# Twelve matmuls on a zero tile, placed in TensorE's waits between the attention steps of the first block

## The chip, the cores and the metric

The kernel runs on one core of one Trainium2 chip. The traces show five engines of it, which run side by side (busy for 95, 41, 38 and 22% of the first span below, the fifth only issues) and wait for each other: TensorE (PE: matmuls, and PEld: its weight loads), VectorE (DVE), ScalarE (ACT), GpSimd (POOL) and SyncE (SP, which issues the transfers). The metric is the device time of one launch in microseconds (us), and lower is better. "Span" is the length of one profiled execution from its first to its last instruction; in the pairs below it is about 1.8 us shorter than the time.

## The reference

The input is q, k, v of 8 batches, 8 heads, 576 positions, 64 columns. Attention is done in chunks of 64 positions, and its result goes through a bilinear feed-forward layer:

```python
scores = scale * np.matmul(q_c, k_c.transpose(0, 1, 2, 4, 3))   # chunks of 64
attn = softmax(scores)
x = np.matmul(attn, v_c)          # as 4608 tokens x 512
out = ((x @ w_a) * (x @ w_b)) @ w_out      # w_a, w_b: 512 x 1536, w_out: 1536 x 512
```

## The kernel before

Tokens are handled in 9 blocks of 512, each of two units of 256. A unit of attention is a chain of steps: transposes of q and k, `scores`, exp on ScalarE, `sums` (a matmul by ones), ln and exp(-x) on ScalarE (the reciprocal of the sum), `values`, and a multiply on VectorE that writes the tile xT. The projections of a block (`ab_step`) read xT. In the steady state attention of a later unit is woven between the projections of an earlier block. For block 0 there is nothing to weave it into: both of its units must be done first, and each step waits for another engine.

```python
def ab_step(K, ft, c0=0, c1=BLK):
    ...
    for n in ("wb", "wa"):
        ps[n] = bank()[:, :c1 - c0]
        for kt in range(NKT):                       # 4 matmuls, 128x512 for a whole block
            nc.tensor.matmul(ps[n], w_ab[n, i][:, kt, o:o + 128], xT[:, kt, c0:c1],
                             start=(kt == 0), stop=(kt == NKT - 1))
    ...
# the start of the program, in the order in which each engine runs it
for i in range(NWP - 1):
    cast_ab(i)                 # POOL casts a pair of weight tiles
    if i < 2:
        load_ab(i + 3)
scores(0)
transpose_pe(1)
sums(0)
scores(1)
values(0)
sums(1)
values(1)
load(2, "qk")
load_ab(5)
...
cast(2, "qk")                  # POOL; unit 2's transposes need it
cast_ab(5)
...
for ft in range(NFT):          # block 0, 12 steps of 8 matmuls
    ab_step(0, ft)
    if ft == 7:
        transpose_pe(2)
    if ft == 8:
        slot(2)                # scores of unit 2
    if ft == 10:
        slot(None, 2)          # sums and values of unit 2
```

The softmax here doesn't subtract the row's maximum and nothing guards it: scores larger than these inputs give would overflow.

## Time and profile before

| | before |
|---|---|
| time, median of the first 3 runs | 330.01 us (329.94 to 330.35) |
| span of the profiled execution | 329.1 us |
| TensorE busy | 311.4 us, 95% |
| block 0's first projection matmul starts | 19.65 us |
| from there to the recorded rise of the clock, at 24.19 us | 4.54 us |

The first two lines are from part 1 and part 4 of the profile's page (busy time of each engine; the chain of work that ended last, by engine). The third is the page's row of granted TensorE clock over 40 slices of the span.

```profile
PE 311.4 (95%) x2712; PEld 157.4 (48%) x2712; DVE 133.9 (41%) x209; ACT 126.7 (38%) x224; POOL 73.7 (22%) x76
...
PE 93%; ACT 3%; DMA 1%; DVE 1%; issue 0%; SPq 0%
...
PEclk9999999999999999999999999999999999999999
```

TensorE is the engine to look at, and it is nearly always busy. So one looks at when it waits, and at how fast it goes. Below, the waits of TensorE: who ended the wait, the total in us, how often, the longest.

```profile
PE ps L156 <- DVE q_raw L144: 5.4, 1, 5.4
PE ps L278 <- DVE xT L239: 3.8, 2, 2.7
PE ps L186 <- ACT qkt L164: 1.6, 2, 1.4
```

The longest xT wait, 2.7 us, is the one just before block 0. The timeline of TensorE shows it in place. The columns are start, duration from the first start to the last end, line, output and inputs, shapes, number of instructions, and in brackets the idle time before and what ended it.

```profile
11.72 0.64 PE L201 MATMUL ps<-E,ones 64*64 64x512 bf16 x4
13.59 0.64 PE L186 MATMUL ps<-qkt 64*64 64x64 bf16 x32 [1.23 <-DVE qkt L164]
...
15.36 1.12 PE L201 MATMUL ps<-E,ones 64*64 64x512 bf16 x4 [0.70 <-ACT E L194]
...
19.65 1.87 PE L278 MATMUL ps<-xT,wb_162 128*128 128x512 bf16 x4 [2.74 <-DVE xT L239]
21.31 1.91 PE L278 MATMUL ps<-xT,wa_164 128*128 128x512 bf16 x4
23.02 1.61 PE L278 MATMUL ps<-xT,wb_162 128*128 128x512 bf16 x4
24.47 1.03 PE L278 MATMUL ps<-xT,wa_164 128*128 128x512 bf16 x4
25.33 1.03 PE L278 MATMUL ps<-xT,wb_170 128*128 128x512 bf16 x4
...
35.69 0.61 PE L156 MATMUL ps<-identity,q_raw 128*128 128x128 bf16 x8
...
36.58 1.03 PE L278 MATMUL ps<-xT,wb_186 128*128 128x512 bf16 x4
...
45.99 0.60 PE L278 MATMUL ps<-xT,wb_162 128*128 128x256 bf16 x4 [1.11 <-DVE xT L239]
```

Read the starts, not the durations: the groups overlap (the one at 19.65 lasts 1.87 us, and the next starts 1.66 us after it). The groups of four at 19.65, 21.31 and 23.02 are 1.66 to 1.71 us apart, which is 0.42 to 0.43 us for each matmul. From 24.47 on the groups are 0.86 us apart, 0.216 us each. Same shape, same operands, half the rate. The clock row says 9 (that is 90% or more) throughout and does not show this. The trace also keeps a list of the changes of the granted clock. It begins here only at 24.19 us, with a rise to full speed, and the clock row counts what lies before the first entry as full: it gives 1.00 from 20.8 to 24.2 us, where the matmuls are 0.42 to 0.43 us apart. Times of a rise or fall of the clock below are entries of that list.

### The profile page before, as it was taken

The numbers are of one execution on the slowest core, as the hardware profiler recorded it, in microseconds if no ns is written. First come the engines' busy times: TensorE is split into PE (matmuls) and PEld (weight loads), VectorE is DVE, ScalarE is ACT, GpSimd is POOL, SyncE is SP. The second block draws the span as 40 slices with busy tenths as digits, with TensorE's granted clock in tenths as the row PEclk, the third lists the DMA queues.
The fourth block names the chain that finished last, engine by engine and source line by source line (L and its number), as shares of the span: only waits on it lengthen the run. The fifth ranks groups of instructions, "written<-read, shape, count | busy, mean of one in ns | idle before, by whom it ended". The sixth has DMA issues, their size and how long they took to land.

```text
span 329.1 us, 6671 instructions
## 1 busy us (share of the span) xinstructions
PE 311.4 (95%) x2712; PEld 157.4 (48%) x2712; DVE 133.9 (41%) x209; ACT 126.7 (38%) x224; POOL 73.7 (22%) x76
## 2 busy tenths in 40 slices
PE   2669989999999999999999999999999999999994
PEld 1424558776444444444444444444444444444441
DVE  3423454554443434343434343444344434433331
ACT  1633567257352525252525252525252524212200
POOL 1575556632222232132232211200000000000000
PEclk9999999999999999999999999999999999999999
DMA  8999899998979998999988918911120112012114
GB/s 241 320 383 293 225 371 257 276 214 197 173 198 248 228 224 192 225 210 253 203 207 211 231 34 147 241 31 34 42 54 3 34 34 64 1 32 63 35 32 96
DMA packets 139166, 53.91 MB, mean 164 GB/s; under 512 B 114560, under 2 KB 132992, under 8 KB 139136
## 3 DMA queue, kind: packets, MB, share of 16 engines
q1 hardware_dynamic: 139136, 53.49, 68.2%
q8 instruction: 21, 0.34, 0.4%
q14 instruction: 9, 0.07, 0.1%
HBM read 37.75 MB, written 9.44 MB: 143 GB/s over the span
## 4 chain that ended last, share of the span: by engine, by line
PE 93%; ACT 3%; DMA 1%; DVE 1%; issue 0%; SPq 0%
PE ps L278 57%; PE ps L294 28%; PE ps L201 2%; PE ps L156 2%; PE ps L186 2%; PE ps L230 1%; DMA k_in<-in_k_dram 1%; ACT rs L216 1%; ACT ln L212 1%; ACT qkt L164 1%; DVE xT L239 0%; DVE k_raw L144 0%; DVE o_sb L302 0%; ACT E L194 0%; SPq L129 0%
## 5 line engine op out<-in xcount | busy, mean ns | idle before, releaser
L286 ACT CAST b_sb<-ps 128x512 bf16<-128x512 f32 (+1 forms) x120 | 64.4, 546 | 142.6 <-PE ps L278 141.4
L287 DVE TENSOR_TENSOR ab_sb<-ps,b_sb 128x512 bf16<-128x512 f32 (+1 forms) x120 | 75.6, 637 | 94.1 <-PE ps L278 89.7
L294 PEld LDWEIGHTS <-ab_sb 128*128 128x128 bf16 x432 | 42.3, 98 | 50.1
L302 DVE COPY o_sb<-ps 128x512 f32<-128x512 f32 x36 | 24.9, 692 | 56.8 <-PE ps L294 56.8
L239 DVE TENSOR_TENSOR xT<-ps,rs 128x512 bf16<-128x512 f32 x36 | 23.4, 687 | 32.3 <-ACT rs L218 27.6
L144 POOL CAST q_raw<-q_in 128x1024 bf16<-128x1024 f32 x17 | 17.7, 1042 | 60.3 <-DMA q_in<-in_q_dram 52.0
L212 ACT ACTIVATE ln<-ps 128x512 f32<-128x512 f32 x36 | 19.9, 596 | 26.4 <-PE ps L201 26.4
L144 POOL CAST k_raw<-k_in 128x1024 bf16<-128x1024 f32 x17 | 17.7, 1042 | 47.9 <-DMA k_in<-in_k_dram 47.7
L278 PE MATMUL ps<-xT,wb_162 128*128 128x512 bf16 (+1 forms) x80 | 20.2, 378 | 3.8 <-DVE xT L239 3.8
L144 POOL CAST v_raw<-v_in 128x1024 bf16<-128x1024 f32 x18 | 18.8, 1042 | 17.7 <-DMA v_in<-in_v_dram 13.3
L294 PE MATMUL ps<-wo_437,ab_sb 128*128 128x512 bf16 x72 | 21.4, 379 | 0.0
L294 PE MATMUL ps<-wo_443,ab_sb 128*128 128x512 bf16 x72 | 21.4, 379 | 0.0
L294 PE MATMUL ps<-wo_433,ab_sb 128*128 128x512 bf16 x72 | 21.4, 379 | 0.0
L294 PE MATMUL ps<-wo_439,ab_sb 128*128 128x512 bf16 x72 | 21.4, 379 | 0.0
L294 PE MATMUL ps<-wo_441,ab_sb 128*128 128x512 bf16 x72 | 21.4, 379 | 0.0
L294 PE MATMUL ps<-wo_435,ab_sb 128*128 128x512 bf16 x72 | 21.4, 379 | 0.0
L194 ACT ACTIVATE E<-ps 128x512 bf16<-128x512 f32 x36 | 19.3, 587 | 1.8 <-PE ps L186 1.8
L278 PE MATMUL ps<-xT,wa_164 128*128 128x512 bf16 (+1 forms) x80 | 19.7, 370 | 0.0
L278 PE MATMUL ps<-xT,wb_186 128*128 128x512 bf16 (+1 forms) x80 | 18.9, 359 | 0.0
L278 PE MATMUL ps<-xT,wb_170 128*128 128x512 bf16 (+1 forms) x80 | 18.9, 359 | 0.0
L278 PE MATMUL ps<-xT,wb_182 128*128 128x512 bf16 (+1 forms) x80 | 18.8, 358 | 0.0
L278 PE MATMUL ps<-xT,wb_409 128*128 128x512 bf16 (+1 forms) x80 | 18.8, 358 | 0.0
(60 smaller groups left out, 324.5 us busy)
## 6 DMA issues: line engine op xcount, KB each, us to landing
out_dram<-o_sb SPq DMA_DIRECT2D x72, 128.0 KB, 2.4
v_in<-in_v_dram SPq DMA_DIRECT2D x32, 256.0 KB, 4.2
q_in<-in_q_dram SPq DMA_DIRECT2D x23, 256.0 KB, 3.9
k_in<-in_k_dram SPq DMA_DIRECT2D x23, 256.0 KB, 3.7
wst<-in_moe_w_b_dram SPq DMA_DIRECT2D x6, 512.0 KB, 7.3
wst<-in_moe_w_a_dram SPq DMA_DIRECT2D x6, 512.0 KB, 8.0
wst<-in_moe_w_out_dram SPq DMA_DIRECT2D x6, 512.0 KB, 7.2
q_in<-in_q_dram SPq DMA_DIRECT2D x4, 512.0 KB, 5.3
```

The source lines that it names most:

```text
L144: eng.tensor_copy(out=raw[n, U], in_=staged.pop((n, U)))
L156: nc.tensor.transpose(tp[:, i, m, :], src[:, i, 2 * m:2 * m + 2, :].rearrange("p j d -> p (j d)"), identity,)
L186: nc.tensor.matmul(sc[j][cl * 64:cl * 64 + 64, m, g, :], t[j * 64:j * 64 + 64, 1, g, m, cl * 64:cl * 64 + 64], t[j * 64:j * 64 + 64, 0, g, ...
L194: nc.scalar.activation(out=E_of[U][:, j], in_=sc[j], func=AF.Exp, scale=scale)
L201: nc.tensor.matmul(sm[cl][j * 64:j * 64 + 64, :], ones[cl * 64:cl * 64 + 64, :], E[cl * 64:cl * 64 + 64, j].rearrange("p m g s -> p (m g s)"),
L212: nc.scalar.activation(out=ln[:, cl].rearrange("p m n -> p (m n)"), in_=sm[cl], func=AF.Ln)
L239: nc.vector.tensor_tensor(out=x_tiles[K][:, :, c0:c0 + 128], in0=av[cl].rearrange("p m g s -> p m (g s)"), in1=rs[:, cl], op=MULT,)
L278: nc.tensor.matmul(ps[n], w_ab[n, i][:, kt, o:o + 128], xT[:, kt, c0:c1], start=(kt == 0), stop=(kt == NKT - 1),)
L286: nc.scalar.copy(out=b_sb[:, :c1 - c0], in_=ps["wb"])
L287: nc.vector.tensor_tensor(out=ab_tiles[K][:, ft, c0:c1], in0=ps["wa"], in1=b_sb[:, :c1 - c0], op=MULT)
L294: nc.tensor.matmul(o_ps, ab_tiles[K][:, ft, tg * 128:tg * 128 + 128], w_out[ft], start=(ft == 0), stop=(ft == NFT - 1),)
L302: nc.vector.tensor_copy(out=o_sb, in_=o_ps)
```

## The change

The intent is to keep TensorE's clock up through the waits of block 0's attention, so that block 0's projections begin at full speed. The result of the added matmuls is read by nobody. `bank()` takes one of the program's eight PSUM buffers, in which matmuls leave their results. In the prediction below, "cold" means at the slow rate and "warm" at the fast one.

```diff
+    warm_in = consts.tile([128, 512], BF16)
+    nc.gpsimd.memset(warm_in, 0.0)
+    warm_ps = []
+    def keep_warm(n):
+        if not warm_ps:
+            warm_ps.append(bank())
+        for _ in range(n):
+            nc.tensor.matmul(warm_ps[0], identity, warm_in, start=True, stop=True)
@@
         sums(0)
+        keep_warm(3)
         scores(1)
         values(0)
+        keep_warm(2)
         sums(1)
         values(1)
+        keep_warm(7)
         load(2, "qk")
```

## The prediction

> **What bounds the kernel.** TensorE: 311.4 of 329.1 us busy (page, part 1), 93% of the chain that ended last. Its waits (waits view, TensorE) sum to 13.1 us, all before 19.65 us but for 1.1 us at 45.99. So from block 0 on it is a TensorE stream; time is saved only by starting block 0 sooner or streaming it faster.
>
> **The slack aimed at.** Block 0's first matmuls (128x512) start 0.43 us apart (timeline: groups of four at 19.65, 21.31, 23.02). From 24.47 us the same instruction goes every 0.216 us. About eleven run at half speed, until about 24.2 us. Shapes and buffers are the same, so it is the array's clock, although the granted-clock row says 1.00 throughout. [...]TensorE idles 2.74 us before 19.65 (waiting for xT), then is slow for 4.6 us. Cost: (24.2-19.65)/2 = 2.3 us, all critical.
>
> **What the change adds.** Twelve 128x512 matmuls (0.43 us each cold, 0.216 warm), a PSUM bank held until block 0, a Pool memset in Pool's idle stretch (1.3-7.7 us). Against the old timeline:
> - Three after the sums of unit 0: 12.36 to 13.64, into a wait that ended at 13.59 (DVE copies). Delay at most 0.1 us.
> - Two after the values of unit 0: 14.7 to 15.55. The sums of unit 1 began at 15.36, but their second matmul needs the second exp, done at 15.80. No net delay.
> - Seven after the values of unit 1 (16.9): until 19.9 cold, 18.4 warm, into the wait until 19.65. The ScalarE chain (16.47 to 19.60) is untouched. Delay 0 to 0.25 us.
> - The held bank makes half of unit 0's values wait for a ScalarE ln ending about 14.16: about 0.1 us.
>
> With them TensorE is nearly continuously busy from 11.7 us[...]. Attention before it is bound by ScalarE and DVE and gains 0 to 0.2 us; block 0 starts at about 19.5 and streams at 0.216 us from its first matmul.
>
> **What is given back.** With block 0 about 2.2 us early, transposes of unit 2 (35.69 before) move to 33.5, while k_raw of unit 2 is cast until 34.12 (POOL timeline, DMA-fed): about 0.3 us stall. The last wa cast ends at 38.08 against a need at 39.2; v_raw of unit 2 at 39.89 against 40.4; w_out at 55.6 against 62. These hold, narrowly. Net gain about 2.0 us.
>
> **Prediction:** 328.0 us, 8 in 10 between 327.2 and 329.5. Faster by over 2%: 0.01; within 2%: 0.98; slower by over 2%: 0.01.
>
> **What would show it.** Right: block 0's first matmuls 0.216 us apart; busy time at the projection line about 2.3 us lower; block 0 begins at 19.4 to 19.8; a small new wait on k_raw at unit 2's transposes; everything after 46 us about 2 us earlier. Wrong: matmuls still 0.43 us apart after 19.65 (zeros or gaps don't count as activity; then 330.0 to 330.3); a slow stretch until about 21 (then 328.7); or the seven push block 0 past 19.9.
>
> **What could make it wrong.** [...]A new wait in block 0 for weights or loads could eat more than 0.3 us, since DMA is saturated until about 66 us.

"Before it" means before full speed. 2.3 us of slow matmuls, taken as about 2.2 us by which block 0 runs ahead, and less about 0.3 us of stall, came to about 2.0 us, from about 330.0 to 328.0 us. "Saturated" is the DMA share in the trace of the kernel before, as the windows view counts it: 1.11 from 9 to 27 us, 1.03 from there to 50 and 1.08 to 66, then 0.95 to 80.

## The result, and the profile after

| | before | after |
|---|---|---|
| time, median of 6 runs | 330.22 us (329.94 to 331.31) | 329.15 us (328.76 to 330.31) |
| ratio of fast runs | | 0.9965, 95% interval 0.9942 to 0.9987 |
| span of the profiled execution | 329.1 us | 327.5 us |
| block 0's first projection matmul starts | 19.65 us | 19.38 us |
| q transposes of unit 2 start | 35.69 us | 33.19 us |
| projections after those transposes start | 36.58 us | 35.02 us |
| block 1's first projection matmul starts | 45.99 us | 44.43 us |

All ratios here are the mean time of one kernel's fast runs over the mean time of the other's fast runs of the same rounds, so they are not quite the ratios of the medians. All timed runs quoted here count as fast, except one of **early_dma**, which is named there.

The lines that answer to those of before. First the page, then TensorE's waits, then its timeline (in the changed file the lines of the same code are numbered 12 higher; line 79 is the added matmul).

```profile
PE 311.8 (95%) x2724; PEld 157.2 (48%) x2724; DVE 133.9 (41%) x209; ACT 126.6 (39%) x224; POOL 74.0 (23%) x77
```

```profile
PE ps L290 <- DVE xT L251: 2.4, 2, 1.3
...
PE ps L168 <- POOL k_raw L156: 0.8, 1, 0.8
```

```profile
12.24 1.32 PE L79 MATMUL ps<-warm_in,identity 128*128 128x512 bf16 x3
13.56 0.45 PE L198 MATMUL ps<-qkt 64*64 64x64 bf16 x32
...
14.22 0.60 PE L79 MATMUL ps<-warm_in,identity 128*128 128x512 bf16 x2
...
16.38 1.69 PE L79 MATMUL ps<-warm_in,identity 128*128 128x512 bf16 x7
19.38 1.02 PE L290 MATMUL ps<-xT,wb_164 128*128 128x512 bf16 x4 [1.32 <-DVE xT L251]
20.24 1.03 PE L290 MATMUL ps<-xT,wa_166 128*128 128x512 bf16 x4
...
33.19 0.61 PE L168 MATMUL ps<-identity,q_raw 128*128 128x128 bf16 x8
34.56 0.62 PE L168 MATMUL ps<-identity,k_raw 128*128 128x128 bf16 x8 [0.76 <-POOL k_raw L156]
35.02 1.03 PE L290 MATMUL ps<-xT,wb_188 128*128 128x512 bf16 x4
...
44.43 0.60 PE L290 MATMUL ps<-xT,wb_164 128*128 128x256 bf16 x4 [1.11 <-DVE xT L251]
```

Busy time hardly moved, 311.4 to 311.8 us: twelve matmuls came in, and the slow ones of block 0 became fast. In the timeline block 0's groups are 0.86 us apart from the very first. The seven matmuls before block 0 are fast too (1.69 us for seven) and end long before xT is there. At 33.19 us TensorE is 2.50 us ahead of before. But then a wait stands at 34.56 that was not there before: the k transposes of unit 2 wait 0.76 us for the cast of k_raw on POOL. From start of the q transposes to the next projections it took 0.89 us before (35.69 to 36.58) and takes 1.83 us now: 0.94 us are given back. What is left, 1.56 us, arrives at block 1, and 1.64 us at the end of the span. The pair of traces flatters the change a little: the profiled execution of the kernel before took 330.88 us, 0.4 us above the mean of its timed runs, and that of the changed kernel 329.24 us, close to its mean.

The cast itself, in POOL's timeline of the kernel before and then of the changed kernel:

```profile
33.08 1.04 POOL L144 CAST k_raw<-k_in 128x1024 bf16<-128x1024 f32 x1 [0.97 <-DMA k_in<-in_k_dram]
```

```profile
33.47 1.04 POOL L156 CAST k_raw<-k_in 128x1024 bf16<-128x1024 f32 x1 [1.38 <-DMA k_in<-in_k_dram]
```

In both it waits for its input transfer. It did not come earlier when TensorE did; in this pair it came 0.39 us later.

### The profile page after: what moved, and what is told of

The parts are those of the page before. It is cut to its first block, busy times and chain, and to the rows that moved or that the text cites. A ratio compares the mean times of both kernels' runs of the same rounds, so it can differ in the third digit from the quotient of the medians.

```text
span 327.5 us, 6696 instructions
## 1 busy us (share of the span) xinstructions
PE 311.8 (95%) x2724; PEld 157.2 (48%) x2724; DVE 133.9 (41%) x209; ACT 126.6 (39%) x224; POOL 74.0 (23%) x77
## 4 chain that ended last, share of the span: by engine, by line
PE 87%; DMA 5%; SPq 5%; ACT 1%; POOL 1%; issue 1%; DVE 0%; POOLq 0%
PE ps L290 53%; PE ps L306 28%; DMA k_in<-in_k_dram 2%; DMA wst<-in_moe_w_a_dram 2%; SPq L141 2%; PE ps L213 2%; SPq L129 2%; PE ps L198 2%; PE ps L242 1%; PE ps L168 1%; SPq L89 1%; ACT rs L228 0%; ACT ln L224 0%; POOL k_raw L156 0%; POOL wa_174 L97 0%
## 5 line engine op out<-in xcount | busy, mean ns | idle before, releaser
L156 POOL CAST v_raw<-v_in 128x1024 bf16<-128x1024 f32 x18 | 18.7, 1040 | 17.5 <-DMA v_in<-in_v_dram 16.8
L290 PE MATMUL ps<-xT,wb_164 128*128 128x512 bf16 (+1 forms) x80 | 18.8, 358 | 2.4 <-DVE xT L251 2.4
L290 PE MATMUL ps<-xT,wb_188 128*128 128x512 bf16 (+1 forms) x80 | 18.9, 359 | 0.0
L290 PE MATMUL ps<-xT,wb_172 128*128 128x512 bf16 (+1 forms) x80 | 18.9, 358 | 0.0
L290 PE MATMUL ps<-xT,wb_424 128*128 128x512 bf16 (+1 forms) x80 | 18.8, 358 | 0.0
L290 PE MATMUL ps<-xT,wb_184 128*128 128x512 bf16 (+1 forms) x80 | 18.8, 358 | 0.0
L290 PE MATMUL ps<-xT,wb_180 128*128 128x512 bf16 (+1 forms) x80 | 18.8, 358 | 0.0
```

The lines of the kernel that those rows point to most:

```text
L156: eng.tensor_copy(out=raw[n, U], in_=staged.pop((n, U)))
```

## The experiments

Theory A, the author's estimate, which the two traces so far allow but don't show: TensorE gets full speed after some microseconds in which it was busy (in the kernel before, 4.54 us into the unbroken stream of block 0), and short waits after that do not take it away; the zero matmuls fill such a stretch. Rival B: what counts is only that TensorE is busy right up to block 0. Theory C: the part of the gain that is missing was given back as the wait on k_raw. Rival D: that stage is short of transferred bytes as a whole, so the wait will only move. Twelve runs were made, in three calls; those of one call ran on one chip and share the runs of the kernel before. Each call had another chip; the medians of the kernel before were 330.48, 330.90 and 330.55 us there, so times from different calls are compared below only with that caution. All results were correct.

### First call: the change again, its parts, and unit 2 one step later

**again** is the changed kernel itself.

> The changed kernel once more, as the yardstick of this call. Theory A[...]: block 0's matmuls 0.216 us apart from the first one, block 0 starts at 19.4 us, ratio to the kernel before 0.9955 to 0.9975.[...]

Measured: 329.04 us median (328.69 to 329.68), ratio 0.9953 (0.9937 to 0.9969). Block 0 began at 19.43 us at full rate, and the wait on k_raw was 0.64 us. The scores of unit 1, at 13.59 us, were fast in both traces (0.45 us), so full speed came at about the same place in these two (13.29 and 13.11 us). In others below it did not: the rise is at 13.53 us in dma_order, 15.25 in late_t2 and 15.05 in dose20, which run the same code up to there on TensorE. Block 0 was fast from its first matmul in all of these, so the change does not hang on one lucky moment of the rise.

**only3** keeps the first three matmuls:

```diff
         values(0)
-        keep_warm(2)
         sums(1)
         values(1)
-        keep_warm(7)
```

> Only the three matmuls after the first sums are kept, the two and the seven are dropped; TensorE then idles 3.0 us before block 0. Theory A: [...]the array is fast from 13.5 us and stays so[...]; block 0 runs at 0.216 us from the start, ratio as the changed kernel, 0.9955 to 0.9980. Rival B (what counts is that TensorE is busy right up to block 0, so the seven do the work): block 0 starts slow, 0.43 us apart for about 4 us, ratio 0.999 to 1.001.

Measured: 330.83 us median (330.35 to 331.2), ratio 1.0006 (0.9991 to 1.0022): no gain. My version of theory A, that a wait of 3.0 us is harmless, fell here. The trace shows why. Below, the view of stretches: the stretch, its length, busy time (and count) of PE, PEld, DVE, ACT, POOL, then the granted clock, DMA share and GB/s. The stretches are cut, to 0.1 us, in steps of 3.40 us that fit the changes of the granted clock: a rise at 14.1, a fall at 17.5 and a rise at 24.3 us, 3.4 and 6.8 us apart.

```profile
10.70:14.10 3.40, 3.18 (x49) 1.66 (x51) 2.57 (x4) 2.04 (x4) 2.08 (x2) 1.00 1.16 323
14.10:17.50 3.40, 1.50 (x88) 1.13 (x79) 1.29 (x2) 2.88 (x7) 2.02 (x2) 0.99 1.06 361
17.50:20.90 3.40, 1.21 (x3) 0.56 (x4) 1.38 (x2) 1.16 (x3) 2.14 (x3) 0.50 1.08 374
20.90:24.30 3.40, 3.40 (x10) 1.22 (x8) 0.69 (x1) 0.58 (x1) 2.61 (x3) 0.50 1.09 386
```

The clock column counts as 1.00 whatever lies before the first recorded change, so it says nothing on the first stretch; the matmul spacing there was 0.43 us. After that stretch, in which TensorE was busy 3.18 of 3.40 us, the values of unit 0 ran fast (0.46 us at 14.12 us; 0.62 in the kernel before). In the next stretch it was busy for 1.50 us, 44%, and the clock fell to half at 17.5 us, two microseconds before block 0. No idle stretch there was longer than 1.0 us. Block 0 then began slow and was fast only from 24.3 us on, after a stretch with 3.40 of 3.40 us busy, as in the kernel before (24.19 us). All six runs have a mean granted clock of 0.988 or 0.989, so the trace is no exception. Theory A, corrected to what this trace shows: the clock changed at ends of such stretches, up after 3.18 and 3.40 us busy of 3.40, down after 1.50, and it stayed at half after 1.21.

**only7** keeps the last seven:

```diff
         sums(0)
-        keep_warm(3)
         scores(1)
         values(0)
-        keep_warm(2)
```

> Only the seven just before block 0 are kept. Theory A: they run cold, 0.43 us each, from 16.9 to 19.9 us, push block 0 by 0.2 to 0.3 us[...]; ratio 0.996 to 0.999, no better than the three alone. Rival B: as good as all twelve, block 0 fast from its first matmul.

Measured: 329.43 us median (329.16 to 329.65), ratio 0.9963 (0.9948 to 0.9979). Here the profiled execution got full speed without any added matmul, then lost it, and the seven won it back just in time:

```profile
9.10:12.50 3.40, 3.03 (x52) 2.27 (x52) 1.56 (x3) 1.34 (x4) 2.08 (x2) 1.00 1.18 267
12.50:15.90 3.40, 1.20 (x70) 0.85 (x74) 2.28 (x4) 3.19 (x6) 2.08 (x2) 1.00 1.01 339
15.90:19.30 3.40, 3.18 (x41) 1.64 (x42) 1.23 (x2) 2.34 (x4) 2.08 (x2) 0.51 1.09 383
```

It was busy 3.03 of 3.40 us from 9.1 to 12.5 us (transposes and sums of the kernel itself), and ran fast after it; 1.20 us in the next stretch, 35%, and it lost the clock; the seven ran slow from 16.7 us and ended only at 19.5, which delayed block 0 by about 0.1 us against the changed kernel; the clock rose at 19.36 us. The other five runs have a mean granted clock of 1.000 against 0.993 here, so they did not lose it in this way; when they gained it is not shown. B as it was put does not hold either: in the changed kernel TensorE idled for 1.32 us right before block 0, and block 0 was fast. So the seven do most of the work, as B says, but by keeping TensorE busy in the stretch before (3.18 of 3.40 us in this trace), as A says: a mean of 329.42 against 329.07 us for all twelve (each the mean of its six runs).

**late_t2** moves the transposes of unit 2 and its scores one step later in the changed kernel:

```diff
-            if ft == 7:
+            if ft == 8:
                 transpose_pe(2)
-            if ft == 8:
+            if ft == 9:
                 slot(2)
```

> The changed kernel with the transposes of unit 2 and its scores one projection step later, so that the key cast (ended 34.5 us in the changed kernel's trace, 0.76 us after TensorE wanted it) is there in time. Theory C (part of the expected gain is given back as that wait): the wait on k_raw is gone and the ratio falls by 0.0015 to 0.0025 against the changed kernel of this call, to about 0.994 to 0.995. Rival D (the wait is only moved: DMA-fed work is late anyhow): a wait of like size turns up at the later weights or values, ratio unchanged.

Measured: 328.35 us median (328.23 to 328.83), ratio 0.9931 (0.9915 to 0.9947). Against **again** of the same call it is 328.42 / 329.07 = 0.998 in the means. The wait on k_raw is gone although the cast of this execution was later still (it began at 34.14 us). The profiled execution, 328.83 us, was the slowest of the six. In it a part went elsewhere, as D said: the next two lines are TensorE's waits in this trace that the changed kernel does not have.

```profile
PE ps L198 <- DMA qkt<-k_raw: 0.4, 1, 0.4
PE ps L290 <- POOL wa L97: 0.2, 1, 0.2
```

The first is at 78 us, where the scores of unit 6 wait for a transfer that transposes k; the timeline has nothing there in **again**.

### Second call: a control, another cure, and an earlier start

**before_late_t2** is the same move in the kernel before, without zero matmuls.

> Control: the kernel before, without any zero matmuls, with unit 2's transposes and scores one step later. Theory C says that moving them helps only because the changed kernel reaches them before the key cast is done; in the kernel before the cast was done 1.5 us ahead. So ratio 0.999 to 1.001. If moving them alone gives 0.997 or less, the gain of the late version was not the returned wait.

Measured: 330.39 us median (330.0 to 331.02), ratio 0.999 (0.9971 to 1.0008). The move alone is worth nothing that shows, though the interval leaves room for the 0.65 us that it gained in the changed kernel. The trace is sharper: block 1 begins at 45.57 us, 0.42 us sooner than in the first trace of the kernel before, and half of the 0.87 us by which the clock rose sooner (23.32 against 24.19) is 0.43 us. So the move itself gave nothing there. With the wait that vanished in late_t2, and with dma_order below, its gain in the changed kernel is the returned wait, as C says.

**dma_order** leaves unit 2 in its place in the changed kernel, but loads and casts its q and k ahead of the fifth weight pair:

```diff
         for i in range(NWP - 1):
+            if i == 4:
+                cast(2, "qk")
             cast_ab(i)
+            if i == 1:
+                load(2, "qk")
             if i < 2:
                 load_ab(i + 3)
@@
-        load(2, "qk")
         load_ab(5)
@@
-        cast(2, "qk")
         cast_ab(5)
```

> The changed kernel with unit 2 left where it was, but its q and k loads and casts put ahead of the loads and casts of the fifth weight pair. Theory C: the key cast now ends at about 31 to 32 us, the wait on k_raw at 33.2 us is gone, and the fifth weight pair is still in time (needed at about 34): ratio 0.993 to 0.995, as the late version. Rival D (the stage is short of transferred bytes as a whole): a wait of 0.5 us or more appears at the fifth weight pair and the ratio stays at 0.995 to 0.9965.

Measured: 328.4 us median (328.32 to 328.9), ratio 0.9929 (0.9911 to 0.9946). The cast of k_raw now begins at 30.14 us; the k transposes follow the q ones without a wait, and no wait turned up at the weights, against D:

```profile
33.28 0.61 PE L168 MATMUL ps<-identity,q_raw 128*128 128x128 bf16 x8
33.72 0.61 PE L168 MATMUL ps<-identity,k_raw 128*128 128x128 bf16 x8
34.17 1.03 PE L290 MATMUL ps<-xT,wb 128*128 128x512 bf16 x4
```

**early** adds thirteen more zero matmuls before and after the first transposes, with the zero tile, now filled by VectorE ahead of the tile of ones, as the weights too:

```diff
-    nc.gpsimd.memset(warm_in, 0.0)
+    nc.vector.memset(warm_in, 0.0)
@@
-            nc.tensor.matmul(warm_ps[0], identity, warm_in, start=True, stop=True)
+            nc.tensor.matmul(warm_ps[0], warm_in[:, :128], warm_in, start=True, stop=True)
@@
         cast(0, "qk")
+        keep_warm(10)
         transpose_pe(0)
+        keep_warm(3)
```

> The changed kernel with thirteen more zero matmuls: ten before the first transposes, three after them, weights from the zero tile, so TensorE is busy from about 1.2 us. Theory A: [...]the transposes of unit 1 then take 0.9 instead of 1.8 us and block 0 starts 0.5 to 1.0 us earlier, near 18.7. But the k_raw wait grows by the same amount, as it is set by transfers: ratio about 0.995, little better than the changed kernel.

Measured: 329.59 us median (329.08 to 331.61), ratio 0.9969 (0.9944 to 0.9994). The attention chain was in part bound by a slow TensorE: block 0 started at 18.42 us, 1.0 us ahead of **again**. Nearly all of that was taken by the casts on POOL: the wait on k_raw grew from 0.64 to 1.34 us, and the q transposes began 0.25 us after TensorE was free for them, when the cast of q_raw ended (32.42 us). Line numbers are one lower here:

```profile
1.19 3.94 PE L78 MATMUL ps<-warm_in 128*128 128x512 bf16 x10 [1.19 <-DVE warm_in L64]
5.46 0.62 PE L167 MATMUL ps<-identity,q_raw 128*128 128x128 bf16 x8 [0.33 <-DVE q_raw L155]
...
18.42 1.02 PE L289 MATMUL ps<-xT,wb 128*128 128x512 bf16 x4 [1.31 <-DVE xT L250]
...
32.48 0.62 PE L167 MATMUL ps<-identity,q_raw 128*128 128x128 bf16 x8
34.43 0.62 PE L167 MATMUL ps<-identity,k_raw 128*128 128x128 bf16 x8 [1.34 <-POOL k_raw L155]
...
44.30 0.60 PE L289 MATMUL ps<-xT,wb 128*128 128x256 bf16 x4 [1.10 <-DVE xT L250]
```

Block 1 began at 44.30 us, and at 44.36 us in **again**: an earlier start of 1.0 us had come to 0.06 us.

**early_late_t2** is both.

> Both: the early zero matmuls and unit 2 one step later. If transfers and not TensorE set that stage, the late version's slack (about 0.5 us) is used up and a wait of 0.2 to 0.6 us on k_raw or on the fifth weight pair comes back: ratio 0.991 to 0.993, at most 0.6 us better than late_t2 alone.

Measured: 328.45 us median (327.49 to 330.16), ratio 0.9937 (0.991 to 0.9965). In its trace unit 2's k transposes do not wait, and block 1 begins at 42.49 us, but the wait of the scores of unit 6 on the transposing transfer is 0.7 us. The times spread over 2.7 us, and the ratio is not told apart from that of late_t2.

### Third call: the corrected theory put to the test

**first5** keeps the three and the two, and drops the seven:

```diff
         values(1)
-        keep_warm(7)
         load(2, "qk")
```

> Only the three and the two are kept; the seven before block 0 are dropped. Theory A as corrected after only3 ([...]47% lost full speed, 62% kept it): full speed from about 13.3 us, kept by the window up to about 16.7, then the window from 16.7 to 20.1 us is idle but for the first part of block 0, so speed drops again WHILE block 0 runs: its first two to four matmuls 0.216 us apart, then about eight 0.43 us apart, then fast for good. Ratio 0.9985 to 1.001. Rival A'[...]: the idle stretch is 3.0 us, so block 0 stays fast and the ratio is that of the changed kernel, 0.9955.

Measured: 330.14 us median (329.75 to 331.04), ratio 0.9987 (0.9967 to 1.0006).

```profile
9.20:12.60 3.40, 3.26 (x53) 2.40 (x54) 1.61 (x3) 1.34 (x4) 2.08 (x2) 1.00 1.20 276
12.60:16.00 3.40, 2.47 (x77) 1.18 (x78) 2.24 (x4) 3.15 (x6) 2.08 (x2) 1.00 0.97 319
16.00:19.40 3.40, 0.52 (x35) 0.49 (x29) 1.38 (x2) 2.34 (x4) 2.08 (x2) 1.00 1.09 378
19.40:22.80 3.40, 3.35 (x8) 1.13 (x8) 0.00 (x1) 0.59 (x1) 2.08 (x2) 0.51 1.09 385
```

"Window" in the expectation is such a stretch. Its 47% stands for the one of only3 that lost the clock (44% as it is cut above), its 62% for the one from 16.7 to 20.1 us in the first trace of the changed kernel, which kept it (2.08 of 3.40 us, 61% as cut there). As the corrected theory has it, the clock was kept in a stretch with 2.47 us busy, was still at full value through the idle stretch, and fell at the end of that one (0.52 us busy), at 19.48 us, just as block 0 had started (19.45 us). The expectation of two to four fast matmuls was off by the place of the stretch: not one whole matmul ran fast before the fall. The longest wait of this kernel after its first transposes is 2.9 us, and the clock fell; so rival A', by which that wait leaves block 0 fast, is refuted, by **first5** as by **only3** (2.9 us too).

**early_dma** puts the early zero matmuls and the earlier loads of unit 2 together.

> The thirteen early zero matmuls together with the earlier loads of unit 2. Block 0 starts near 18.4 us as in early, unit 2's transposes are wanted at 32.2 us; the key cast in dma_order's trace is done in time for 33.7, by little for 32.6. If it holds, the 1.0 us of the earlier start survives: ratio 0.990 to 0.992, about 327.5 us, better than dma_order. If the weights or the values become late instead, new waits of 0.3 to 1.0 us and a ratio of 0.992 to 0.994.

Measured: 327.82 us median (327.28 to 332.29), ratio 0.9941 (0.9898 to 0.9984). In its trace the early start survives: block 0 at 18.46 us, no wait on k_raw at unit 2 (q at 32.27, k at 32.72 us), block 1 at 42.57 us, a span of 325.5 us. Five of its six runs lie between 327.28 and 328.33 us, which is the fastest of all kernels here; the sixth took 332.29 us, over 1.5% above the fastest. The ratio 0.9941 must count that run: even over the fastest run of the kernel before (330.01 us) the mean of the five fast ones, 327.75, would give 0.993. Over the mean of 330.64 us it gives 0.991, without an interval. The kernel **early** had one run of that kind too (331.61, called fast). Both have a mean granted clock of 0.994, where the other runs of the two kernels have 0.997 to 1.000; that is 1 to 2 us of granted clock less, an estimate (0.003 to 0.006 of a span of about 327 us), so the clock took part, but it does not cover the 4.5 us of the longer one. No trace caught such a run, so its cause is open, and I don't call this version the best.

**dose20** puts twenty instead of seven before block 0.

> Twenty instead of seven before block 0: at 0.216 us each they run from 16.4 to 20.75 us, 1.3 us beyond the wait, so block 0 starts at about 20.8 instead of 19.4. But the wait on k_raw (0.64 us in the changed kernel, about 0.9 us with what goes with it) disappears, as TensorE now comes later than the cast. Net 0.4 to 0.8 us slower than the changed kernel: ratio 0.9965 to 0.9985. If zero matmuls were free beyond the wait, no difference; if the wait were not set by the cast's own time, 1.3 us.

Measured: 329.71 us median (329.64 to 329.77), ratio 0.997 (0.9954 to 0.9986). The zero matmuls ran until block 0's start at 20.76 us, 1.3 us after that of **again**, and the wait on k_raw was gone:

```profile
16.44 4.49 PE L79 MATMUL ps<-warm_in,identity 128*128 128x512 bf16 x20
20.76 1.03 PE L290 MATMUL ps<-xT,wb 128*128 128x512 bf16 x4
...
34.58 0.61 PE L168 MATMUL ps<-identity,q_raw 128*128 128x128 bf16 x8
...
44.88 0.60 PE L290 MATMUL ps<-xT,wb 128*128 128x256 bf16 x4 [1.10 <-DVE xT L251]
```

At block 1 (44.88 us) it is 0.52 us behind **again** (44.36), not 1.3: most of the delay had only replaced a wait. That is C from the other side. And its four times lie within 0.13 us of each other, where the kernel before spread over 1.4 us in the same call.

**before_again** is the kernel before, for a second trace.

> The kernel before once more, for a second trace. Block 0 starts at 19.6 us and slow; [...]the speed-up falls elsewhere than in the first trace (24.2 us)[...]; each microsecond later costs half a microsecond of span against 329.1.

Measured: 330.57 us, span 328.8 us. Block 0 started at 19.68 us, slow. Its third group of four took 1.16 us to the next group (23.05 to 24.21), where the first trace has 1.45 us (23.02 to 24.47). At half rate, 0.29 us less time means that the clock rose about 0.6 us sooner in this execution; its list of changes has the rise at 23.63 us. The span was 0.3 us shorter (328.8 and 329.1), which is the half of that, as expected.

## Why the prediction was right or wrong

- **Range and class: right.** 328.0 us with 327.2 to 329.5 was said; 329.15 us was measured, inside the range but in its upper part.
- **The bottleneck and the slack: right.** Block 0's matmuls went from 0.43 to 0.216 us each from the first on, and TensorE had gained 2.50 us when it reached the transposes of unit 2 (2.2 us were expected). Of these, 0.27 us came from an earlier start of block 0, within the 19.4 to 19.8 us that were named, but for 0.02 us. Busy time of the projection line fell by 2.2 us (197.1 to 194.9; about 2.3 was said). The full clock itself came at 13.29 us, sooner than I had expected: the 3.40 us before it, all of them busy, began at 9.9 us and held the kernel's own transposes and sums too.
- **Cost of the twelve: right.** They lie in waits. dose20 shows what happens when they don't.
- **The term that was mis-sized: "about 0.3 us stall" at unit 2's transposes.** It measured 0.94 us in the first trace (0.76 us of it shown as the wait), and 0.64 us of wait in **again**. Two things add up: TensorE came 0.3 us sooner than I reckoned, and the cast came 0.39 us later than in the one trace that I had read its time from. The cast's start is no fixed number: over the twelve traces of kernels in which the order of loads was left alone it lies between 32.56 and 34.14 us, without a clear difference between kernels with a fast and a slow block 0. I had read one value and treated it as certain. late_t2 and dma_order, which remove this wait, bring the gain in the means to 2.2 and 2.3 us (330.61 less 328.42, and 330.78 less 328.47), about the size that I had put on the clock alone.
- **"Everything after 46 us about 2 us earlier": 1.56 us** in the trace, for that reason. The gain in the means of the timed runs was 1.2 us in the first comparison (330.47 less 329.31) and 1.5 us in the second (330.61 less 329.07).
- **"Zeros or gaps don't count as activity": half right as a danger.** Zeros count: in early, after ten matmuls with both operands zero from 1.19 us on, the q transposes at 5.46 us took 0.62 us, against 1.03 us in the kernel before. Gaps count against it, and sooner than I thought when I planned only3: the clock fell after stretches with 1.50 (only3), 1.20 (only7) and 0.52 (first5) of 3.40 us busy. How much is enough is not shown: 2.08 of 3.40 us kept full speed in the changed kernel (16.7 to 20.1 us), and 2.21 of 3.40 did not bring it in the kernel before (14.0 to 17.4).
- **Differences between executions**. The kernel before ranged from 329.91 to 331.59 us over the first comparison and the three calls, 1.68 us. If the rise can fall anywhere within the 3.4 us that lie between two clock changes in only3, the time that block 0 loses at half rate differs by up to 1.7 us: an estimate from that distance and from the 0.43 and 0.216 us of a matmul. In the three traces without added matmuls (before, before_again, before_late_t2) the clock rose at 24.19, 23.63 and 23.32 us, 4.54, 3.95 and 3.65 us after block 0's first matmul, and the spans are 329.1, 328.8 and 328.6 us. In each the clock fell again near the end, 303.8 us after the rise (in before at 327.98 us). A run's mean granted clock counts the half clock from that fall to the end of the span (1.14 us in before, which makes 0.998), so it tells when the clock rose: the later the fall, the higher the mean. The 33 timed runs of the kernel before in the three calls sort by it: two runs at 0.997 took 329.91 and 329.96 us, eight at 0.998 took 330.26 to 330.69, fourteen at 0.999 took 330.90 to 331.59. The other nine, at 0.986 or 0.987, took 330.01 to 330.55; so low a mean fits a clock that was gained before block 0 and lost again, as in only7's trace, but no trace of the kernel before shows it. Some kernels that reach block 0 at full speed and don't wait for the cast hardly spread (dose20 0.13 us; late_t2 five of six within 0.25 us); early_late_t2, whose trace shows the same two things, spreads over 2.7 us, and why is open.

Best of what ran, with a narrow spread: dma_order (ratio 0.9929) and late_t2 (0.9931), which the intervals don't tell apart; the five fast runs of early_dma are faster still (0.991), but one run in six is not. All keep the twelve matmuls. Against the changed kernel, late_t2 is 0.2% faster in the means.

## What to carry to other kernels

If the same matmul runs at half the rate early in a program, look at the spacing of its starts, and ask how busy TensorE was in the few microseconds before; filling waits with unused matmuls can win back what the slow stretch costs (here about half of its length), but here only where the wait just before the real work was filled too (only3 and first5, which left 2.9 us of it empty, had ratios of 1.0006 and 0.9987, with 1 inside both intervals), and not beyond its end (dose20 began block 0 1.3 us later). When a change brings one stage forward, list what that stage will meet sooner, and take the arrival of transfers from several executions, as a range. A gain that is smaller than expected may lie one wait further on, where a reordered load gets it back.
